# Block products of a softplus feed-forward in the second half of d_ff only, and the staging of block sums moved to other storage

## The chip, the cores and the metric

One core of a Trainium2 chip runs the whole program. The metric is the device time of one execution in microseconds; the kernel before took 651.81 us in the median of three runs (650.3 to 656.61).

## The reference, cut to what matters

The input is q, k and v of 4 batches, 8 heads, 768 positions and 64 channels, and two weight matrices, 512 x 2048 and 2048 x 512, in 64-bit floating point.

```
k_sum = k.reshape(B, H, nb, 32, D).max(axis=3)
v_sum = v.reshape(B, H, nb, 32, D).mean(axis=3)
scores = concat(masked q k^T / 8 (only |i - j| < 16), q k_sum^T / 8 + log(32))
a = softmax(scores)
x = a @ concat(v, v_sum)             # 3072 tokens x 512
h = x @ w_in                         # 512 -> 2048
out = softplus(h) @ w_out            # 2048 -> 512
```

Each row attends to its neighbours within 15 positions and to 24 block sums (maxima of keys, means of values). The result goes through a feed-forward with softplus.

## The kernel before, in words

**Tokens.** The 3072 tokens are 12 chunks of 256 (three to a batch), and two chunks make a group, so there are six groups, x = 0 to 5, of 512 tokens. Attention is done in units of one chunk and two pairs of heads, four units to a group: scores (line 643), masking and row minimum on VectorE (656), exponentials on ScalarE (664), normalizing (677 or 680), a transposition that goes by 32 x 32 squares on VectorE (710), out to DRAM (718) and back (722), and the values' product (741). The result is copied from PSUM to r (753), and r is kept in DRAM for the second pass (616). Group 0 has a path of its own, with transposition on TensorE (697) and its queries and values in the storage s0 to s3.

**Two passes over d_ff.** The 2048 hidden channels are 16 blocks f of 128. Since the weights of only half of them fit, groups 0 to 4 first run through f = 0 to 7 (first pass) and put a partial output in DRAM (1219); group 5 runs through all 16 blocks, during which the second half of the weights is loaded and converted; then groups 4, 3, 2, 1, 0 run through f = 8 to 15 (second pass), adding their partial output (1207). For the second pass the kept r is loaded again (1295).

**Precision.** Every operand is split in a high and a low part that TensorE can multiply at its full rate, and each product is three: high x high, high x low, low x high. The weights come as pairs of 32-bit words and are turned to a high and a low part by bit operations (lines 934 to 977), eight steps to a tile, partly in temporaries.

**Hidden products, two ways.** Plain (`hidden`, 1051): per block f, 4 parts of 128 input channels x 3 terms = 12 matmuls of 512 columns (1060). As blocks (`hidden_pair`, 1077): two f blocks and the two chunks make a 2 x 2 matrix of 2 x 2 blocks, multiplied with seven products in place of eight. Each product is 2 x 3 = 6 matmuls of 256 columns (1100), 42 for a pair of f against 24 of 512 columns. For that, sums of weight blocks are made once per pair of f (`sums_of_weights`, 983: lines 1000, 1008 to 1011, 1024, 1031; four sums, then high and low part, storage s0 to s3), seven operands are made for each group (`prepare`, 848: four differences, 811 and 812, and seven splits, 796 and 803), and the products are combined by a copy p (1119 or 1120) and seven additions or subtractions on VectorE (1110). A pair holds both PSUM banks of the ring "ph" until its softplus has read them; a plain hidden product takes one of these two banks, and so does the values' product of an attention unit (735).

`WHOLE = 2` says from which group on the first pass works as blocks: groups 0 and 1 are plain (`prepare_whole`, 815: high and low part of r, 827 and 834), groups 2 to 5 and the whole second pass are as blocks. This makes 16 plain blocks f and 40 pairs.

After either, softplus is taken twice by ScalarE from PSUM (1162 rounded to the high part gh, 1166 exact), VectorE makes the low part gl (1170), and 12 matmuls of 512 columns per f add to the output (1177).

**Storage.** Tiles are taken from rings by tag. The ring "t" has two buffers and holds, in the order of use, key and value rows for block sums (`Sums.declare`, 369: kf and st, four loads of 384 KB each per batch), temporaries of the weights, temporaries of the weights' sums, and outputs on their way out. s0 to s3 hold group 0's queries and values, then some temporaries of weights and one tile of group 1, then the weights' block sums.

**Order.** Every piece of work is a task with a number, given in the order in which the program adds tasks. `SEQUENCE` (147) lists these numbers in the order in which they are issued; a letter picks another engine for a task. Each engine and the DMA queue of SyncE works its tasks strictly in that order, and a task waits for its operands and for its storage.

Of the kernel before, what the change touches and what calls it, by code (L numbers as in the profile page):

```python
# [147 lines left out]
162 163a 0 1 3 4 5 6 7 8 64 153 154a 2 313 43 155 156 164 165 157 51 68 9 10 11 12 13 14 15 16 17 18 19 158a 20 21 22  # L148
23 24 45 44 46 53 47 152 25 167 55 166 69 49 26 159 27 28 29 30 160 31 171 32 33 34 168 57 35 161a 169 36 37 52 38 72
59 73 39 40 54 48 180 86 87 61 170a 56 58 100 74 104 75 50 172 76 88 189 60 77 173 41 79 78 70 181 89 315 314 66 174  # L150
65 182 62 80 90b 63 175 71 67 101 321 312 176 316 183 198 199 106 185 105 184 108 109 103 107 42 177 110 122 190 194
123 191 111 112a 192 102 124 193 81 91 93 324 92 186 187a 94 343 82 95 136 325 178 84 125 179 85 83 96 345 98 99 195
97 196a 113 326 126 140a 146a 200a 204 188 327 197 201 202 203 205 115 342 208 114 116 117 344 137 328b 127 346 372
374 351a 129 329 138 118 128 354 119 130 317 355 236 213 120 131 132 320 322 134 133 121 330 135 390 375 209a 246 373
210 211 389 356 357 376 247 255 393 248 212 217 331 391 249 143a 392 250 256 251 332 377 257 218 252 206 214 262 147a
318 319 207 215a 358b 398 333 263 237 401 258 359 259 264 265 402 334 253 266 323 219a 254 378 227 382 238a 260 220
221 403 139 222 360 261 239 335 420 419 269 270 240 216a 241 336 267 268 421 347 352 242 348 404 149 228a 276 271 379a
232 384 272 422 383a 229 380 405b 349 274 277 230 338 350 231 223 361 273 278 385 362 406 423 363 353 141 279 364 386
283 381 284 280 233 234 275 224 428a 235 407 431 285 340 365 533 286 534 287 394 290 225 291 532 366 537a 142 408 432
387a 409 388 411 515a 297 516a 399 243 395 298 433 226 397 410 368 400 292 396 293 369a 540 434 557 244 558 435a 281  # L160
299 300 436 282 561a 556 294 520 541 437 517a 148 412 370a 288 245 367 542 301 518a 413 417 424 289 564 427 543 429
438 425 430 440 521a 441 371a 544b 519 439 426 522 418 339a 581 589a 523a 580 582 295 296 302 583 303 304 442 545 415
584 565 416 443 341 756 445 546 446 535 447 757 760 566 567 448a 592 449 761 547 450 451 452 548 536 610 549 612 550
568 458 306a 307 611 150 144 453 309a 305 618a 613 569 459 593 538 460 310 461 308 465 539 609 466 462 524a 467 468
454 469 455 594 525 595 311 596 551 570 145 552 768 571 621 559 472 572 769 554 456 555a 526a 597 562 473 474 573 560
774 479 527a 480 574 563 553 775 475 622 476 773 598 457 481 482 463 483 575 776 486 764 777 782 585 464 588 758 623
487 624 470 591 625 488 489 586 587 599 785 590 471 765 576a 601 600 602 626 786 490 762 627 787 477 759 603 604a 802
803 493 804 606 801 500 501 763a 810 788 494 614 789a 805 766 578 579 615 767 790 607 628 495 620 502 496 617 813 629
770 619 814 616 478 630 608 484 497 631 151 503 485 414 605 815 1053 632 771 577 504 633a 640 637 635 816 643 491 641
638 642 830 644 1054 639a 492 1055 645a 791 829 831 636 646 647 337 1057 778 652 649 650 648 651 653 654 655 657 834a  # L170
772 659 784 817b 656 779 792 837 658 498 1056 661 528 818 855 660 662 444 838 663 854 859 668 499 856 783 529 669 505
670 793 507 673 1058 508 819 780 839 679 840 862 841a 509 781 997 998 842 1001 675 530 1000 843 676 506 863 674 999
682 664 510 677 864 683 511 794 680 531a 678 512a 684 795 1006 685 513a 514 665 686 688 687 1061 865 681 689 866a 693
1065 690 694 666 667 671 1009 695 867 796 797 1010 1026 1029 1027 1028 1025 672 1062 806 820 868 698 701 811 704 1011
1034 823 699a 700 702 703 822 705 709 707 807 821 812 711 710 708 1012 706 713 712 691 714 1066 1013 799a 718 719 715
808 720 809 692 696 798 824 1059 1063 1037 1014 825 832 723 726 833 725 1038 724 727 1071 729 728 1079 732 730 734
827a 828a 1074 835 844 846 735 736 733 845 836 731 847 738 737 1072 1070 739 743 740 697 716 744 745 800 1073 1015 848
869 1082 857 717 1060 1064a 858 872 721 870 871 1100 849a 1108a 861 722 741 742 1039 860 1040 826 873 1041 1042 850
851 852 853a 1103 1083 1016 1019 874 1043 876 881 884 748 878 882 883 1101 885a 879a 880a 877 886a 1017 1099 887 746
888 896 890 893 753 891 898 894 1084 897 899 750 902 889 1102 892 747 1085 900 903 751a 901 895 1086 909 1002 1111 904  # L180
910 875 1004 749 1008 911 905 1003 1018 1087 906 914 754 917 916 920 915a 918 921 1005 919 922 925 923 907 924 926
1246 755 1247 927 929 930 1007 928 931 908 934 912 935 1067 936 1020 1112 1251a 1068a 913 1021 1248 1023a 1044 1069
1030 1047 1033 939 942 940 943 1036 941 945 948 950 946 944 952 951 949 954 955 1035 1046 1032 953 1045 947 634 1031
956 959 932 960 961 933 1088 1048 1113 1075 1049a 1254 1024 1089 1270 964 967 965 1114 970 1090 1076 1092 968 966 971
1115b 752 1080 975 969 1078 973 976 974 979 977 980 937 1077 978 1274 1091 1022 938 957 1116 972 981 984 985 1081 986
1271 1117 1255 1093 1051a 1269 1050 1094a 958 1118 1052 1120 1121 1104 1119 1096 1256 1107 1277 1097 962 1257 1110
1105 963 982 1258a 1259 1278 1106 1109 1095 1122 1098a 1293 1260 1294 1296 1249 1123 1130 983 1124 1125 1295 1127 1133
1131 1128 1132 1250 1129 1134a 1126 1135a 987 1292 1261 1136 1137 1142 1145 1139 1138 1146 1279 1140 1252 1143 1147
1141 988 1301a 1148 1264 1149 991 1150 1280 989 1262 1253 1304 1151 1152 1281 990 1144 1263 1158 1153 1154 1159 1160
994 992 1265 1266 1155 995 1282 1283 1321 1323 1284 1285 1163 996 1166 993 1286 1676 1305 1169 1164a 1167 1170 1174  # L190
1172 1173 1165 1175 1324 1156 1168 1157 1306 1178 1171 1176 1177 1272 1307 1161 1179 1183 1320 1329 1308 1162 1184
1180 1185 1322 1188 1191 1275 1189 1190 1267a 1309 1192 1273 1194 1193 1195 1287 1199 1197 1200 1310 1198 1203 1268a
1201 1276 1204 1202 1196 1208 1209 1205 1181 1210 1332 1288 1297 1303 1289 1182 1311 1333 1213 1219 1214a 1216 1217
1679 1215 1334 1218 1222 1220 1224 1299 1314 1313 1335 1302 1226 1225 1223 1227 1298 1300 1677 1228 1229 1221 1336
1186 1312 1233 1234 1678a 1187 1206 1290a 1337 1230 1235 1338 1315 1316a 1207 1211 1680 1212 1231 1682 1232 1238 1325
1339 1340 1317a 1326 1681 1327 1342 1291 1318 1341 1331 1328 1330 1343 1344a 1319a 1683a 1350 1345 1236 1239 1351 1347
1348 1353 1352 1349 1354a 1355a 1346 1356 1357 1686 1362 1365 1359 1360 1243 1358 1363 1361 1820 1367 1458 1369 1476
1366 1240 1684 1368 1370 1371 1372 1364 1378 1373 1379 1380 1237 1244a 1374 1459 1477 1383 1478 1386 1384 1385 1389
1813 1245 1481 1685a 1241 1387 1479 1460 1390 1392 1394 1388 1396 1480 1375 1376 1463 1692a 1393 1395 1398 1377 1391
1381 1695a 1482 1399 1397 1403 1494 1461 1404 1462 1400 1405 1408 1464 1483 1689 1484 1411 1410 1465 1466 1551a 1409a  # L200
1412 1495a 1414 1382 1417 1816 1552a 1499 1467 1415 1413 1242 1419 1472 1468a 1496 1485 1418 1421 1401 1420 1422 1402
1416 1423 1406 1428 1497 1407 1553 1424 1498 1469 1429 1554 1425 1430 1433 1490 1513 1555 1503 1470 1504 1514a 1436
1435 1434 1439 1500 1501 1471 1502a 1486a 1518 1515 1516 1442 1437 1505a 1440 1444 1438 1441 1445 1443 1426 1487 1446
1532 1448 1517 1810 1427 1449 1506 1519 1447 1431 1450 1453 1454 1455 1568 1571 1556a 1520 1569 1570 1507 1574 1572
# [40 lines left out]
def kernel(  # L245
# [33 lines left out]
    NG = 2  # L279
# [1078 lines left out]
```

## Time and profile before

| | |
|---|---|
| median of three runs | 651.81 us (650.3 to 656.61) |
| profiled execution | 652.5 us, span 650.7 us |
| mean granted TensorE clock | 0.979 |
| PE busy | 608.9 us, 94%, 4812 matmuls |
| VectorE busy | 444.8 us, 68% |
| ScalarE busy | 351.0 us, 54% |
| GpSimd busy | 199.3 us, 31% |
| DMA | 104.46 MB, mean 161 GB/s |

The span runs from the first to the last instruction. A matmul's end is modelled, so PE's busy time is more than what TensorE needs; the distance from start to start in a full stream says more. A row of a view names the line, engine, operation, the tile written and the tiles read, the count, then busy time and mean duration, and the idle time of the engine right before, with what ended it.

### The profile page before, as it was taken

What the parts mean: (1) busy time and instruction counts of PE and PEld (TensorE: products, weight loads), DVE (VectorE), ACT (ScalarE), POOL (GpSimd) and SP (SyncE); (2) the same over time, 40 slices, a digit from 0 to 9 for tenths busy, and PEclk for the clock granted to TensorE, in tenths of its full rate; (3) what the DMA queues carried; (4) which work ended last, traced back from release to release, by engine and by line L of the source; (5) the groups of instructions that cost most, each with busy time, mean ns of one, the idle gap of its engine ahead of it and who ended that gap; (6) DMA issues with size and microseconds to landing.
All of it is one profiled execution on the core that took longest, in us unless ns stands there. A gap on an engine that the chain in (4) does not pass through costs nothing.

```text
span 650.7 us, 13005 instructions
## 1 busy us (share of the span) xinstructions
PE 608.9 (94%) x4812; PEld 522.0 (80%) x4812; DVE 444.8 (68%) x1150; ACT 351.0 (54%) x852; POOL 199.3 (31%) x168
## 2 busy tenths in 40 slices
PE   8559889898999989999999999999999999999997
PEld 7357667676778778878978987889899898999895
DVE  4978799646888567686659999986655455455442
ACT  3979789694886363768525877742312313123220
POOL 5325155252741231011144474332230233401000
PEclk9979989898999989999999999999999999999999
DMA  9998997989977964686554742023102140040121
GB/s 288 265 269 245 259 236 220 266 240 259 289 246 235 231 204 129 208 252 196 165 154 138 259 156 95 1 66 130 48 17 98 65 150 14 1 130 1 53 79 64
DMA packets 88960, 104.46 MB, mean 161 GB/s; under 512 B 27488, under 2 KB 67008, under 8 KB 88128
## 3 DMA queue, kind: packets, MB, share of 16 engines
q1 hardware_dynamic: 88896, 103.62, 54.1%
q8 instruction: 38, 0.62, 0.4%
q14 instruction: 26, 0.21, 0.1%
HBM read 73.92 MB, written 27.26 MB: 156 GB/s over the span
## 4 chain that ended last, share of the span: by engine, by line
PE 60%; DMA 15%; DVE 10%; SPq 6%; ACT 4%; issue 2%; POOL 2%; DVEq 0%; POOLq 0%; ACTq 0%
PE po L1177 26%; PE hx L1100 14%; PE hy L1100 10%; PE ph L1060 3%; DMA squares<-tb 3%; DMA st<-v_hp_dram 3%; PE xo L741 2%; ACT sp L664 2%; SPq L722 2%; PE sc L643 2%; DMA v<-v_hp_dram 2%; PE warm L1251 2%; DMA raw<-w_in_dram 1%; DMA first<-v_hp_dram 1%; DMA raw<-w_out_dram 1%
## 5 line engine op out<-in xcount | busy, mean ns | idle before, releaser
L1177 PE MATMUL po<-w,gh 128*128 128x512 f32 x768 | 204.5, 394 | 1.9 <-ACT gh L1162 1.7
L1177 PEld LDWEIGHTS po<-w,gh 128*128 128x128 f32 x768 | 139.6, 188 | 31.5 <-ACT gh L1162 3.0
L1177 PE MATMUL po<-w,gl 128*128 128x512 f32 x384 | 117.1, 399 | 1.0 <-DVE gl L1170 1.0
L803 POOL TENSOR_TENSOR x<-r,x 128x512 fp32r<-128x512 f32 x35 | 48.8, 1400 | 189.6 <-DVE x L796 98.7
L1162 ACT ACTIVATE gh<-hx 128x512 fp32r<-128x512 f32 x40 | 23.9, 598 | 121.7 <-DVE hx L1110 121.6
L1177 PEld LDWEIGHTS po<-w,gl 128*128 128x128 f32 x384 | 70.4, 189 | 16.9 <-DVE gl L1170 1.8
L1100 PE MATMUL hx<-x,w 128*128 128x256 f32 x480 | 71.7, 286 | 4.2 <-ACT p L1119 3.5
L1100 PE MATMUL hx<-x,sw 128*128 128x256 f32 x480 | 71.8, 286 | 3.2 <-DVE u L1110 1.6
L1100 PEld LDWEIGHTS hx<-x,w 128*128 128x128 f32 x480 | 65.6, 190 | 10.3 <-ACT p L1119 5.0
L664 ACT ACTIVATE sp<-sp,nm 128x120 f32<-128x120 f32 x192 | 73.0, 382 | 0.2
L1100 PEld LDWEIGHTS hx<-x,sw 128*128 128x128 f32 x480 | 63.9, 191 | 5.4 <-DVE u L1110 2.5
L1100 PE MATMUL hy<-x,sw 128*128 128x256 f32 x480 | 66.5, 284 | 0.0
L963 POOL TENSOR_TENSOR t<-t,raw 128x1024 int32<-128x1024 int32 (+1 forms) x20 | 43.6, 2192 | 70.7 <-DVE t L949 31.0
L1100 PEld LDWEIGHTS hy<-x,sw 128*128 128x128 f32 x480 | 61.5, 190 | 0.6 <-DVE sw L1031 0.2
L1060 PE MATMUL ph<-xw,w 128*128 128x512 f32 x192 | 51.2, 421 | 0.0
L656 DVE CUSTOM_DVE_ANT_0 sp<-sc,added 128x120 f32<-128x120 f32 x192 | 40.8, 278 | 10.8 <-PE sc L643 9.6
L1060 PEld LDWEIGHTS ph<-xw,w 128*128 128x128 f32 x192 | 38.2, 203 | 9.7 <-DVE gl L1170 0.3
L796 ACT CAST x<-r 128x512 fp32r<-128x512 f32 x37 | 22.8, 619 | 34.2 <-PE hx L1100 11.2
L677 POOL TENSOR_TENSOR sp<-sp,ss 128x960 f32<-128x960 f32 x11 | 20.0, 1815 | 68.9 <-DVE ss L672 51.6
L1110 DVE TENSOR_TENSOR u<-hx,p 128x256 f32<-128x256 f32 x40 | 16.9, 424 | 32.7 <-ACT p L1119 27.1
L1110 DVE TENSOR_TENSOR u<-hy,u 128x256 f32<-128x256 f32 x80 | 30.9, 419 | 11.8 <-PE hy L1100 11.1
L1170 DVE TENSOR_TENSOR gl<-hy,gh 128x512 fp32r<-128x512 f32 x40 | 27.5, 688 | 13.7 <-ACT hy L1166 13.6
(108 smaller groups left out, 974.8 us busy)
## 6 DMA issues: line engine op xcount, KB each, us to landing
squares<-tb SPq DMA_DIRECT2D x20, 512.0 KB
pT<-squares SPq DMA_DIRECT2D x80, 128.0 KB
raw<-w_out_dram SPq DMA_DIRECT2D x16, 512.0 KB
kf<-kT_dram SPq DMA_DIRECT2D x16, 384.0 KB
raw<-w_in_dram SPq DMA_DIRECT2D x6, 1024.0 KB
q<-qT_dram SPq DMA_DIRECT2D x20, 256.0 KB
raw<-r SPq DMA_DIRECT2D x20, 256.0 KB
part<-ob SPq DMA_DIRECT2D x10, 512.0 KB
```

The lines of the kernel that those rows point to most:

```text
L656: nc.vector.tensor_tensor_reduce(out=sp()[:, n], in0=unit(n), in1=added()[:, kinds.index((lows[w], lows[w + 1]))], scale=-SCALE, scalar=FL ...
L664: nc.scalar.activation(sp()[:, n], sp()[:, n], AF.Exp, bias=nm()[:, n:n + 1], scale=-1.0, accum_out=ss()[:, n:n + 1],)
L677: engine.tensor_tensor(sp(), sp(), s, op=ALU.mult)
L796: copy(out=to(0), in_=a())
L803: engine.tensor_tensor(to(1), a(), to(0).bitcast(F32), op=ALU.subtract)
L963: nc.gpsimd.tensor_tensor(a, a, word(0, I32), op=ALU.add)
L1060: nc.tensor.matmul(ph(), lhsT=lhs(part, cc), rhs=xw[cc][0]()[:, xw[cc][1], a], start=cc == 0 and n == 0, stop=cc == NCC - 1 and n == 2,)
L1100: nc.tensor.matmul(to()[:, half], lhsT=lhs(wa, cc), rhs=of_x(xa)[:, cc * CH:(cc + 1) * CH], start=cc == 0 and m == 0, stop=cc == NG - 1 an ...
L1110: DVE, dve(CH), lambda: nc.vector.tensor_tensor(out(), a(), b(), op=op), reads, [write],
L1162: nc.scalar.activation(gh(), all_of(), AF.Softplus)
L1170: nc.vector.tensor_sub(out=gl(), in0=all_of(), in1=gh().bitcast(F32))
L1177: nc.tensor.matmul(po[t](), lhsT=a()[:, t * P:(t + 1) * P], rhs=w2()[:, part, i2 * DM:(i2 + 1) * DM], start=f == f0 and i == 0, stop=f == ...
```

## The change

Groups 2 to 5 do their first-pass blocks plain, and group 5 all 16 of its blocks; only the second pass of groups 4 to 0 (five groups) works as blocks. The block sums of the first half's weights are no longer made. Group 5 isn't copied to r: its high and low parts are taken from PSUM, as for group 0. The plain operands alternate between two sets of storage by the parity of the group. The key and value rows for the block sums move from ring "t" to s0 to s3, one buffer each, and temporaries of weights that were there move to "t" and "x0". `SEQUENCE` is replaced by a new one of 2099 tasks in place of 2348.

```diff
-    WHOLE = 2
...
-                kf = buffer([P, S], F32, "kf", "t", T_BUFS, dynamic=True)
-                st = buffer([P, n_t, P], F32, "st", "t", T_BUFS, dynamic=True)
+                kf = buffer([P, S], F32, "kf", tag=f"s{i % 2}", pool=wts, bufs=1)
+                st = buffer([P, n_t, P], F32, "st", tag=f"s{2 + i % 2}", pool=wts, bufs=1)
...
-        if x not in x_bufs and not x:
+        if x not in x_bufs and not x % 2:
             x_bufs[x] = [(buffer([P, 1, 2, CT], F32R, "xw", tag=f"x{3 + cc}", bufs=1), 0) for cc in range(NCC)]
         elif x not in x_bufs:
-            x_bufs[x] = [(buffer([P, 1, 2, CT], F32R, "xw", tag=f"x{1 + cc}", bufs=2), 0) for cc in range(NG)]
-            both = buffer([P, NG, 2, CT], F32R, "xw", tag="s3", pool=wts, bufs=1)
-            x_bufs[x] += [(both, g) for g in range(NG)]
+            x_bufs[x] = [(buffer([P, 1, 2, CT], F32R, "xw", tag=f"x{1 + cc % 2}", bufs=2), 0) for cc in range(NCC)]
...
-        if x:
+        if x and x < NX - 1:
             r = block(2 * i + hp // NG)
...
-            (1, 0): ("tb", work, 1), (1, 1): ("x0", work, 2), (2, 0): ("x0", work, 2),
-            (2, 1): ("s0", wts, 1), (3, 0): ("s1", wts, 1), (3, 1): ("s2", wts, 1),
+            (1, 0): ("x0", work, 2), (2, 0): ("x0", work, 2), (3, 0): ("x0", work, 2),
...
-        pairs = x >= WHOLE or f0 > 0
+        pairs = f0 > 0
...
                 if x < NX - 1:
                     keep(x, n, r[n])
-                if x < WHOLE:
                     prepare_whole(x, n, r)
-                else:
-                    prepare(x, n, r)
...
-        if x == WHOLE and not f0:
-            for f in range(0, HALF, 2):
-                sums_of_weights(f)
-        if x == NX - 1:
-            sums = attend(x, sums)
-        elif x and not f0:
+        if x and not f0:
             sums = attend(x, sums)
```

More of the change, by code (lines that the diff above doesn't have):

```diff
@@ L153 @@
[L153 to L162, printed above, removed]
@@ L233 @@
[L233 to L234 removed]
[6 rows of a table removed]
+0 3 4 162 43 1 5 6 51 7 44 8 9 10 11 12 13 14 15 16 17 18 19 20 21 22 23 24 25 26 27 28 29 30 31 32 33 153 45 47 68
+154a 158a 34 155 163a 64 46 52 156 53 55 164 2 157 165 167a 72 54 35 57 189 69 36 159 59 160a 161 49 73 48 37 86 313
+61 166 56 74 171 87 190 38 39 168 75 58 40 191 88 41 60 104 62 100 76a 172a 50 152 321a 180 192 176a 77 79 66 316 65
@@ new lines @@
+173 174 63 67 169 42 78 108 71 175 80 170 70 177 314 315 185 194 101 109 89 312 193 110 122 123 81 324 208 198 181a
+103 90b 124 107 105 343 111 82 195 84 344 182 209a 91 102 136 106 196a 112a 346 183 199 184 92 93 94 95 325 83 213
+178a 197 85 342 113 125 326 372 345 96 186 210 211 114 179 351 212 138 115 116 98 117 99 97 376 126b 127 317 118 120
+327 214 200a 129 128 215a 130 354 137 217 131 373 246 218 380 328 329 134 330 140 132 121 141 355 133 320 119 135 201
+247 319 356 248 390 255 249 392 393 331 223a 357 187 389 334 332 318 374 322 333 391 202 204 250 256 257 188 262 203
@@ new lines @@
+412 437 524 541 546a 424 370 543 426 300 244a 438 288 341a 525 245 147a 440 289 301 429 427 441 295 339 413 439 549
+430 296 425 526 567 417 369 527 303 568 569 305 570 528 550 304 529 442 697 518 415 522 309 443 416a 302 447a 371a
+418a 571 445a 448 446 576a 519 551 521 530 142 533 552 306a 449 450 532 553 451 458 531 459 452 453 554 579 597 598
+600 307 599 460 601 454 699 455 555 456 695 461 580 606a 465 466 581 694 467 462 534 609 711 698 714 556 310a 457 535a
+558 713 544 582 144 696 468 719a 710 583a 584 463 610 559 469 611 537 612 464 705 470 548 700 557 712 547 613a 545 414
@@ new lines @@
+986 873 976 1120 1117 874 1115 1100 1013 869 692 870 875 988 876 765 1014 1000 1003 913 1123 946a 989a 1101 993 1140
+1016 945 851 1015 857 915a 1427 917a 1428 1561 877 1562 858 864 865 871 872 994 1102 991a 878 1017 1002 1103a 1005
+1143 1001 992 947a 1104 1124 1006 881 1018 1148a 880 879 1563 1019a 990 1142 1105 1021a 1022a 1125 882a 1023a 1433
+1139 1024 1141 1025 1026 1094 1027 1028 1151 1034 1029 1035 1095 1030 1041 1567 1042 883 1167 1036 1106 1107 1037 1043
+1109 1038 1168 1020 1108 1048 1170 1097 1126 1127a 1044 1049 1098 1050 1051 885 1045 1110 1128 1031 1113 1111 1171
@@ new lines @@
+1169 886a 1118 1129 1052 1130 1152 1153 1112 1114 1131 1032 1122 1033 1055 1154 1056 1062 1057 943 1133 1119 1155 1058
+1063 1039 1132 1040 1429a 1046 1176 1179 1156 887 1121 1064 1437 1059 1134 1047 1065 1157 1066 1180 1135 1181 1182
+1183a 884 1137 1144 1150 1158 1160 1136 1146 1145 1149 1053 1069 1161 1159 1147 1070 1054 1060 1071 1072 1434 1138
+1162 1184 1163 1073 1061 1185 1076 1165 1571 1077 1078 1166 1440 1441a 1067 1068 1079 1080 1172 1173 1186 1568a 1074
+1075 1081 1085a 1187 1164 1174 1084 1083 1177 1188 1178 1175 1438 1088 1439a 1442 1189 1190 1193 1191 1194 1082 1192
@@ new lines @@
+1086a 1087 1195 1196 1197 1198 1204 1205 1206 1089 1199 1207 1253 1254 1208 1574 1211 1200 1212 1271 1272 1218 1219
+1276 1201 1213 1273 1214 1289 1220 1221 1274 1255 1202 1215 1225 1203 1275 1277 1278 1226 1256 1257 1258 1222 1232
+1262 1290 1227 1233 1291 1279a 1209 1228 1210 1259 1216 1260 1261 1308 1263a 1292 1264 1267 1346 1294 1234 1235 1229
+1293 1347a 1295 1296a 1217 1265 1309a 1266 1223 1310 1280 1268 1224 1298 1299 1313 1239 1236 1430 1300a 1281 1240 1230
+1241 1282 1701 1311 1242 1285 1231 1312 1283 1269 1246 1348a 1243 1284 1247 1237 1248 1238 1249 1314 1090 1327 1250
@@ new lines @@
+1541 1539 1540 1542 1534 1499 1696 1546 1500 1572a 1576 1519 1543 1547 1520 1548 1579a 1581 1582 1573 1697a 1583 1589
+1585 1584a 1586 1592 1524 1587 1588 1593 1594 1590 1596 1595 1591 1597 1598 1605 1705 1525 1544 1545 1549 1702 1703a
+1599 1600 1606 1607 1704 1610 1611 1616 1613 1550 1612 1614 1615 1617 1618 1619 1552 1620 1554 1551 1558 1623 1555
+1621 1622 1601 1624 1625 1559 1626 1630 1602 1603 1835 1829 1627 1631 1699 1604 1632 1608 1635 1708a 1711a 1638 1636a
+1639 1641 1637 1646 1640 1642 1839 1556 1644 1647 1645 1648 1650 1649 1643 1609 1651 1655 1656 1652 1657 1700 1628
@@ new lines @@
+1872 1893 1892 1894 1895 1898 1899 1900 1903 1906 1904a 1905 1909 1907 1908 1912 1910 1914 1913 1915 1918 1916 1919
+1876 1877 1911 1917 1920 1923 1924 1925 1976a 1896 1968 1928 1931 1929 1934 1930 1932 1939 1828 1980a 1933 1941 1937
+1982a 1897 1974a 1935 1940 1901 1977 1938 1978 1943 1936 1955 1902 1921 1983 1975a 1944 1942 1984a 1948 1981a 1945
+1949 1950 1985 1988 1987 1986a 1824 1989 1991 1996 1922 1990 1998 1959 1994 1992 1999 1995 1997 1993 2000 2001 1926
+1927 2002 2007 2008 2009 1946 2012 2013 1947 1952 1957 2018 2015 2014 1951 2016 2019 2023 2021 1953 2017 1956 2020
@@ L241 @@
+2022 2025 1954 2003 2024 1960 2004 2026 1961 2027 2028 2032 2033 2029 2005 2006 2034 2037 2040 2039 2038 2041 2043
+2046 2048 2042 2044 2047 2050 1958 1962 2045 2049 2010 2011 2051 2052 2053 2054 2057 2030 2058 2059 2062 2065 2063a
+2068 2064 2066 2067 2031 2073 2071 2069 2075 2074 2072 2077 2078 2076 2079 2035 2036 2070 2082 2089 2083 2084 2094
+2055 2056 2060 2061 2080 2081 2088 2087 2085 2086 2096 2098 2095 2091 2097 2090 2093 2092
 """
```

117 lines of the change are left out of this document (40 added, 77 removed), and 6 rows, old and new, of the table SEQUENCE.

## The prediction

> **What bounds the kernel now.** I read the granted clock and the busy time by stretches first, cut at the places where the kind of work changes: start and first attention (to 53 us), the feed-forward of token groups 0 and 1 (to 172), groups 2 to 4 (to 340), the first half of group 5 (to 430), the dense part (to 632), the tail. The columns are the stretch, its length, PE, PEld, DVE, ACT and POOL busy with their instruction counts, the granted clock, the DMA engines' busy share and GB/s.
>
> ```profile
> core 0: us, PE busy (x) PEld busy (x) DVE busy (x) ACT busy (x) POOL busy (x), PEclk, DMA share, GB/s
> 0.00:53.00 53.00, 38.06 (x573) 30.53 (x574) 36.96 (x142) 36.94 (x126) 21.78 (x37) 0.87 0.98 264
> 53.00:172.00 119.00, 108.41 (x868) 84.40 (x869) 88.42 (x260) 92.64 (x252) 48.73 (x39) 0.96 0.92 253
> 172.00:340.00 168.00, 160.00 (x1487) 137.85 (x1487) 119.45 (x366) 101.44 (x281) 43.63 (x33) 0.99 0.70 206
> 340.00:430.00 90.00, 86.21 (x548) 74.86 (x549) 82.85 (x144) 64.88 (x90) 42.38 (x28) 1.00 0.36 123
> 430.00:632.00 202.00, 202.00 (x1282) 183.03 (x1282) 111.74 (x234) 52.91 (x101) 42.82 (x33) 1.00 0.20 67
> 632.00:650.70 18.70, 14.23 (x64) 11.36 (x62) 5.34 (x9) 2.18 (x4) 0.00 (x0) 1.00 0.15 57
> ```
>
> From 430 to 632 us TensorE never stops, at full clock: there only the amount of matmul work counts. Before 53 us the DMA engines are full (0.98). Between, TensorE has some idle time everywhere, while VectorE reaches 82.85 of 90 us in the fourth stretch. So a change of matmul work is paid in full at the end, and can be paid out of idle time between 53 and 430 us.
>
> How much time is there to be had? Busy time of PE has modelled ends, so I count matmuls and multiply by their spacing in full streams, read from the chain of waits in order of time (start us, length us, what, how many) and, for the scores, from the timeline:
>
> ```profile
> 118.38 5.93 PE ph L1060 x18
> 125.01 4.13 PE ph L1060 x18
> 256.07 1.11 PE xo L741 x32
> 471.35 1.43 PE hx L1100 x12
> 472.78 1.43 PE hy L1100 x12
> ```
>
> ```profile
> 223.87 1.05 PE L643 MATMUL sc<-k,q 64*64 64x120 f32 x32
> ```
>
> A 512-column product takes 4.13 / 18 = 0.229 us, a 256-column block product 1.43 / 12 = 0.119 us, a unit of 32 value products 1.11, a unit of 32 score products 1.05. The first row is the same work just after a wait: 1.8 us more, so a gap of TensorE costs more than its own length. The counts of two stretches, PE alone (count, busy and mean ns, idle before and its releasers):
>
> ```profile
> L1060 PE MATMUL ph<-xw,w 128*128 128x512 f32 x192 | 51.2, 421 | 0.0
> L1177 PE MATMUL po<-w,gh 128*128 128x512 f32 x112 | 30.2, 399 | 1.7 <-ACT gh L1162 1.7
> L1177 PE MATMUL po<-w,gl 128*128 128x512 f32 x52 | 16.0, 402 | 0.5 <-DVE gl L1170 0.5
> L741 PE MATMUL xo<-pT,v 120*64 120x64 f32 x256 | 10.1, 237 | 5.8 <-DMA pT<-squares 2.1 <-DMA st<-v_hp_dram 1.4 <-DMA raw<-r 1.2
> L643 PE MATMUL sc<-k,q 64*64 64x120 f32 x256 | 9.5, 271 | 2.6 <-DMA k<-kT_dram 1.9 <-DMA q<-qT_dram 0.6
> ```
>
> 53 to 172 us: (192 + 112 + 52) x 0.229 = 81.5, 8 units of values 8.9, 8 of scores 8.4: 98.8 of 119 us. Lost: 20.2 us, and the waits named are the attention's (DMA), not the feed-forward's.
>
> ```profile
> L1177 PE MATMUL po<-w,gh 128*128 128x512 f32 x321 | 85.4, 395 | 0.1
> L1177 PE MATMUL po<-w,gl 128*128 128x512 f32 x164 | 49.6, 401 | 0.5 <-DVE gl L1170 0.5
> L1100 PE MATMUL hx<-x,w 128*128 128x256 f32 x243 | 37.0, 288 | 4.2 <-ACT p L1119 3.5 <-DVE u L1110 0.5
> L1100 PE MATMUL hx<-x,sw 128*128 128x256 f32 x240 | 36.8, 289 | 3.2 <-DVE u L1110 1.6 <-DVE hx L1110 1.4 <-DVE x L803 0.2
> L1100 PE MATMUL hy<-x,sw 128*128 128x256 f32 x240 | 34.2, 286 | 0.0
> L1100 PE MATMUL hy<-x,w 128*128 128x256 f32 x120 | 18.0, 286 | 0.8 <-DVE u L1110 0.4 <-DVE hy L1110 0.3
> L741 PE MATMUL xo<-pT,v 120*64 120x64 f32 x384 | 14.3, 225 | 2.4 <-DMA pT<-squares 1.5 <-DMA v<-vs 0.7
> L643 PE MATMUL sc<-k,q 64*64 64x120 f32 x320 | 10.5, 269 | 0.6 <-DMA q<-qT_dram 0.6
> ```
>
> 172 to 430 us: 485 x 0.229 = 111.1, 843 x 0.119 = 100.3, 12 units of values 13.3, 10 of scores 10.5: 235.2 of 258 us. Lost: 22.8 us. Of this, 4.2 + 3.2 + 0.8 = 8.2 us are idle times directly before a block product, nearly all waiting for the copies and sums that block products need (p, u, hx, hy); the attention's waits are only 3.0.
>
> **The change, part by part.** *More matmul work.* 20 of 40 pairs of f blocks (groups 2, 3, 4 with four each, group 5 with eight) become plain. A pair as blocks is 7 products of 6 matmuls, 42 x 0.119 = 5.0 us; plain it is 2 x 12 of 512 columns, 24 x 0.229 = 5.5 us. 20 x 0.5 = **+10.0 us**, on the engine that sets the end. The Trainium skill, "TensorE: Matmul & The Clock Gate", section "Back-to-back issue gap", gives N / 2.4 + 2.5 ns for a matmul in a warm stream: by that, as an estimate, a pair is 42 x 109 = 4.6 against 24 x 216 = 5.2 us, the 20 pairs cost +12, and the time would come out 2 us above my forecast. The same section gives 131 ns per matmul at N = 512 within a real kernel, by which a plain pair would be the cheaper one (24 x 131 = 3.1 us); the 229 ns above contradict it, and I give it no chance.
>
> *Waits that go.* The same 20 pairs lose their combining: seven VectorE operations a pair at line 1110 and one copy of p. All of them lie before 430 us (columns: stretch, length, DVE busy, clock, DMA share, GB/s):
>
> ```profile
> 172.00:340.00 168.00, 34.10 (x84) 0.99 0.70 206
> 340.00:430.00 90.00, 22.52 (x56) 1.00 0.36 123
> ```
>
> 140 operations, 56.6 us of VectorE, and the 8.2 us of waiting for them go with certainty, as no plain product reads p, u, hx or hy. What is late next is the softplus (line 1162) ahead of the output products; in the plain stretch above it cost 1.7 + 0.5 us over 16 blocks.
>
> *Elementwise work that changes.* Groups 2 to 5 are no longer prepared as seven operands with four differences, but as four whole tiles. What is added, 24 halves from r and 8 straight from PSUM (high, low):
>
> ```profile
> L827 ACT CAST xw<-r 128x256 fp32r<-128x256 f32 x7 | 2.7, 403 | 0.1
> L834 DVE TENSOR_TENSOR xw<-r,xw 128x256 fp32r<-128x256 f32 x4 | 1.6, 421 | 0.1
> L771 ACT CAST xw<-xo 128x256 fp32r<-128x256 f32 x8 | 2.8, 376 | 1.7 <-PE xo L741 1.5
> L775 DVE TENSOR_TENSOR xw<-xo,xw 128x256 fp32r<-128x256 f32 x8 | 2.9, 413 | 0.0
> L803 DVE TENSOR_TENSOR x<-r,x 128x512 fp32r<-128x512 f32 x28 | 23.1, 833 | 3.1 <-ACT x L796 3.0
> L811 DVE TENSOR_TENSOR r<-r 128x512 f32<-128x512 f32 x20 | 13.4, 693 | 3.2 <-ACT r L753 2.5 <-POOL x L803 0.4
> L1031 DVE TENSOR_TENSOR sw<-ws,sw 128x1024 fp32r<-128x1024 f32 x5 | 7.1, 1429 | 0.0
> ```
>
> 32 x 0.82 = 26 us are added. Removed are 28 lows at 0.83 or more, 28 highs and 16 differences at 0.69: over 45 us. Four of the eight sets of weight sums (before group 2) go too, each about 1.4 for its low half and more for sums and high half. The chain from the last attention unit of a group to the first hidden product becomes copy, high, low: about 0.6 + 0.4 + 0.4 us, where a block group runs through splits and differences at 0.7 to 0.8 each. And in the fourth stretch the sums of the second half's weights are no longer due within group 5, but one group later, under the dense part.
>
> *The staging.* k and v rows for the sums of batches 1 to 3 leave the ring "t" (two buffers, shared with weight temporaries and stores) for s0 to s3. DMA counts and bytes don't change, nor does what SP issues, only when buffers come free. Now this row stands in the chain of waits:
>
> ```profile
> 45.80 6.98 DMA st<-v_hp_dram
> ...
> 67.72 11.23 DMA st<-v_hp_dram
> ...
> 93.45 0.35 ACT k L525
> ```
>
> The second load was issued only at 67.7, when the ring and SP's order let it. With the DMA engines at 0.92 a load freed earlier pushes another back, so I bound the gain of this and of the missing weight sums in the second stretch between 0 and 8 us and take **-3**. In the other direction, s0 to s3 hold the first group's queries and values until about 53 us, so the first load can come up to 53 - 45.8 = 7 us later than now; its sums are first copied at 93.45, some 40 us on, which hides that as long as the four rounds of loads don't each slip.
>
> *The sum for 172 to 430 us.* Lost there: 22.8. From below 8.2 come back (the waits named); from above 22.8 less the attention's 3.0 and about 2 for the softplus, 18. I take **-15**, nearer to the upper end, because the remaining 14.6 are mostly short slips before products whose operands the saturated VectorE delivers late, and VectorE loses 56.6 us of work in these 258. The start, dense part and tail stay: 0. The written order is a new one throughout; I put nothing on that beyond these bounds.
>
> Sum: +10.0 - 3 - 15 = -8.0 us. The profiled execution took 652.5 us (span 650.7, and 1.8 around it); 652.5 - 8.0 = **644.5 us**. The three runs have a median of 651.81, 0.7 below the profiled one; within that I make no difference. Against the median it is -1.1%; a measurement of this kernel tells about 1% from no change, and that is the bound of my three chances (645.3 and 658.3 us).
>
> **The rivals.** (1) *Only the named waits go* (8.2), nothing comes back from 53 to 172: +10.0 - 8.2 = +1.8, 654.3 us. For it: DMA at 0.92 and 0.70 feeds the attention, whose chain alone could set the pace of groups 2 to 4. Against: TensorE, not DMA, is at 160 of 168 there. Chance 0.25.
>
> (2) *Plain groups run like the plain stretch* (slower). The only plain stretch now gets 98.8 us of products into 119, a share of 0.83. If groups 2 to 4 go at that share, their 168 us, with about 153 of products now (counted as above) and 6 more after, take 159 / 0.83 = 192: +24; with +4 and -6 for group 5, +22, 674 us. The mechanism is attention units on TensorE's queue, whose late pT blocks the hidden products queued behind them. It decides once the DMA share in that stretch nears 0.9; half way it makes 663 us. Against: bytes are the same and the share is 0.70. Chance 0.15.
>
> (3) *All that can come back does*: +10.0 - 8 - 18 = -16, 636.5 us. For it: the relief of VectorE is larger than all of TensorE's loss. Against: loads wait for loads in the second stretch. Chance 0.15.
>
> That the change doesn't do what it says I rule out: `pairs = f0 > 0` is false for all of group 5 too.
>
> **How the numbers follow.** My forecast has 0.45, its own range 640 to 649. It lies on the bound of 1%, about two thirds of it below 645.3. Faster: 0.30 + 0.15 = 0.45; same: 0.15 + 0.22 = 0.37; slower: 0.15 and 0.03 of rival 1 = 0.18. The range reaches from below rival 3 to near the half way case of rival 2: 634 to 661.
>
> **What would show it.** In the changed profile: ph x672 and block products x840 in all; 24 hidden matmuls of a plain pair in about 5.5 us; line 1110 x140 in place of 280; no idle before a hidden product on ACT p or DVE u before the second pass; group 5's stretch without gaps; lost time between first hidden product and dense part down from 43 to about 25 us. It is wrong if that loss stays above 35 us (then the attention set it), or if a plain pair takes other than 5.5 us in a full stream, or if the waits named before output products (line 1177) grow by several us.

## The result, and the profile after

The changed kernel took 629.92 us (median of four runs, 628.99 to 630.68), the kernel before in the same runs 653.95 us: a ratio of 0.9636, 95% interval 0.9577 to 0.9694. The profiled execution took 630.05 us with a span of 628.3 us. The prediction had 644.5 us and a range of 634 to 661: the direction was right, the time lies 4 us below the range, and the gain is nearly three times the one forecast (22.4 us of span in place of 8.0).

The line of busy times on the changed kernel's page, and the busy time by stretches, cut at the same events as before: the first hidden product of the feed-forward, the first of group 2, the first of group 5, the begin of the second pass, the end of the dense part. The columns are those of the prediction.

```profile
PE 609.2 (97%) x4452; PEld 508.9 (81%) x4452; DVE 388.0 (62%) x998; ACT 328.0 (52%) x809; POOL 162.0 (26%) x145
```

```profile
0.00:52.00 52.00, 41.16 (x573) 32.92 (x573) 37.87 (x139) 35.67 (x123) 20.35 (x36) 0.80 1.00 285
52.00:164.00 112.00, 109.30 (x927) 86.04 (x926) 83.18 (x256) 87.01 (x238) 36.79 (x30) 1.00 0.88 252
164.00:324.00 160.00, 158.98 (x1254) 127.65 (x1253) 79.60 (x275) 96.82 (x273) 31.74 (x33) 1.00 0.77 228
324.00:406.00 82.00, 82.00 (x357) 66.66 (x356) 66.50 (x87) 52.36 (x71) 30.57 (x17) 1.00 0.37 127
406.00:610.00 204.00, 204.00 (x1291) 184.77 (x1290) 116.01 (x238) 53.97 (x102) 42.53 (x32) 1.00 0.19 66
610.00:628.30 18.30, 13.75 (x60) 10.91 (x58) 4.87 (x9) 2.18 (x4) 0.00 (x0) 0.99 0.16 57
```

Read against the lines of before: in groups 0 and 1 TensorE is now at 109.30 of 112 us (108.41 of 119), in groups 2 to 4 at 158.98 of 160, in group 5 at 82.00 of 82. Group 5 is without a gap and VectorE has 66.50 of 82 us there, where it had 82.85 of 90.

What TensorE lost is counted as in the prediction, from PE alone in the two stretches, groups 0 and 1 first, then groups 2 to 5 (count | busy and mean ns | idle before and its releasers):

```profile
L1045 PE MATMUL ph<-xw,w 128*128 128x512 f32 x192 | 47.2, 396 | 2.1 <-DVE gl L1155 2.0
L1162 PE MATMUL po<-w,gh 128*128 128x512 f32 x126 | 34.4, 400 | 0.0
L1162 PE MATMUL po<-w,gl 128*128 128x512 f32 x63 | 19.3, 399 | 0.0
L629 PE MATMUL sc<-k,q 64*64 64x120 f32 x288 | 9.7, 270 | 0.5 <-DMA k<-kT_dram 0.5
L727 PE MATMUL xo<-pT,v 120*64 120x64 f32 x256 | 9.4, 225 | 0.1
```

(192 + 126 + 63) x 0.229 = 87.2, 8 units of values 8.9, 9 of scores 9.5: 105.6 of 112 us. Lost: 6.4 us, before 20.2.

```profile
L1045 PE MATMUL ph<-xw,w 128*128 128x512 f32 x480 | 116.7, 394 | 0.0
L1162 PE MATMUL po<-w,gh 128*128 128x512 f32 x306 | 80.5, 394 | 0.0
L1162 PE MATMUL po<-w,gl 128*128 128x512 f32 x150 | 45.2, 399 | 0.0
L727 PE MATMUL xo<-pT,v 120*64 120x64 f32 x384 | 13.8, 225 | 0.1
L629 PE MATMUL sc<-k,q 64*64 64x120 f32 x288 | 9.5, 269 | 1.0 <-ACT gh L1147 1.0
```

936 x 0.229 = 214.3, 12 units of values 13.3, 9 of scores 9.5: 237.1 of 242 us. Lost: 4.9 us, before 22.8.

So the span's -22.4 us is made up of +10.0 for matmuls, -13.8 of lost time in groups 0 and 1, -17.9 in groups 2 to 5, and -1.0 in the start (first hidden product at 51.9 us in place of 52.9); 0.3 is the error of this count.

### The profile page after: what moved, and what is told of

Same layout as the page of the kernel before. It is cut to its first block, busy times and chain, and to the rows that moved or that the text cites. A ratio compares the mean times of both kernels' runs of the same rounds, so it can differ in the third digit from the quotient of the medians.

```text
span 628.3 us, 12022 instructions
## 1 busy us (share of the span) xinstructions
PE 609.2 (97%) x4452; PEld 508.9 (81%) x4452; DVE 388.0 (62%) x998; ACT 328.0 (52%) x809; POOL 162.0 (26%) x145
## 4 chain that ended last, share of the span: by engine, by line
PE 85%; DMA 8%; SPq 3%; ACT 1%; DVE 1%; issue 1%; DVEq 0%; POOL 0%; POOLq 0%; ACTq 0%
PE po L1162 40%; PE ph L1045 21%; PE hx L1085 9%; PE hy L1085 7%; PE xo L727 3%; PE sc L629 3%; DMA raw<-w_in_dram 2%; DMA k<-kT_dram 2%; DMA squares<-tb 2%; PE warm L1236 2%; DMA kf<-kT_dram 1%; DMA q<-qT_dram 1%; DMA v<-v_hp_dram 1%; SPq L708 1%; SPq L523 1%
## 5 line engine op out<-in xcount | busy, mean ns | idle before, releaser
L1045 PE MATMUL ph<-xw,w 128*128 128x512 f32 x672 | 163.9, 395 | 2.1 <-DVE gl L1155 2.0
L1045 PEld LDWEIGHTS ph<-xw,w 128*128 128x128 f32 x672 | 125.6, 188 | 32.5 <-DVE gl L1155 2.8
L1147 ACT ACTIVATE gh<-hx 128x512 fp32r<-128x512 f32 x20 | 12.0, 599 | 114.9 <-DVE hx L1095 114.9
L1155 DVE TENSOR_TENSOR gl<-ph,gh 128x512 fp32r<-128x512 f32 x56 | 38.0, 684 | 40.8 <-ACT ph L1151 39.3
L1147 ACT ACTIVATE gh<-ph 128x512 fp32r<-128x512 f32 x56 | 33.5, 598 | 53.4 <-PE ph L1045 48.5
L650 ACT ACTIVATION_READ_ACCUMULATOR sp<-sp,nm 128x1 f32 x192 | 36.0, 187 | 0.0
L1085 PE MATMUL hx<-x,sw 128*128 128x256 f32 x240 | 35.4, 283 | 0.0
L1085 PE MATMUL hx<-x,w 128*128 128x256 f32 x240 | 35.1, 282 | 0.0
L1085 PEld LDWEIGHTS hx<-x,w 128*128 128x128 f32 x240 | 32.8, 189 | 1.9
L1085 PE MATMUL hy<-x,sw 128*128 128x256 f32 x240 | 33.2, 282 | 0.0
L1151 ACT ACTIVATE ph<-ph 128x512 f32<-128x512 f32 x56 | 32.8, 591 | 0.0
```

Of the source, the lines that this page charges most:

```text
L650: nc.scalar.activation(sp()[:, n], sp()[:, n], AF.Exp, bias=nm()[:, n:n + 1], scale=-1.0, accum_out=ss()[:, n:n + 1],)
L1045: nc.tensor.matmul(ph(), lhsT=lhs(part, cc), rhs=xw[cc][0]()[:, xw[cc][1], a], start=cc == 0 and n == 0, stop=cc == NCC - 1 and n == 2,)
L1085: nc.tensor.matmul(to()[:, half], lhsT=lhs(wa, cc), rhs=of_x(xa)[:, cc * CH:(cc + 1) * CH], start=cc == 0 and m == 0, stop=cc == NG - 1 an ...
L1147: nc.scalar.activation(gh(), all_of(), AF.Softplus)
L1151: nc.scalar.activation(all_of(), all_of(), AF.Softplus)
L1155: nc.vector.tensor_sub(out=gl(), in0=all_of(), in1=gh().bitcast(F32))
```

## The experiments

**The price of a plain pair.** The changed kernel with its second pass plain as well, so that 20 more pairs give up their block products.

```diff
-        pairs = f0 > 0
+        pairs = False
```

The preparation and the weight sums of the second pass go with them.

> The changed kernel with the second pass plain too, so 20 more pairs are plain; no block sums of weights at all. The second pass is a full stream of TensorE, so this measures the price of a plain pair by itself. My prediction's step (0.5 us a pair from the spacing): 640 us, +10. By the formula N / 2.4 + 2.5 ns: 642 us. If a plain pair costs TensorE nothing more: 630 us or less.

642.8 us, 12.9 over the changed kernel; the spans are 641.4 and 628.3 us. 2.1 of these 13.1 us lie ahead of the second pass, which begins at 408.1 us in place of 406.0. From there to the end it takes 233.3 in place of 222.3 us: 11.0 us for 20 pairs, 0.55 each, or a little less, as by the spacing of the products under 1 us of it is lost time. The prediction's 0.5 from the spacing of the products is confirmed to within a tenth. In the dense part nothing hides it. The Trainium skill's formula in "TensorE: Matmul & The Clock Gate", section "Back-to-back issue gap", gave 12 for the same 20 pairs, as an estimate; that section gives it for an isolated matmul with a warm clock, not for a stream. The measurement lies between the two.

**Order alone, or work alone.** Each kernel with the other one's written order, carried over task by task; a task that only one of them has was put beside its neighbour.

> The changed kernel with the written order of before carried over task by task (a plain hidden product stands where the block products of its pair stood). If less elementwise work is what brought TensorE's lost time down (theory 1), the time stays at 630 to 637 us and the loss between the first hidden product and the dense part at 10 to 17 us. If the new written order did it (theory 2), the time is 645 to 655 us and the loss from 53 to 172 us stays near 20 us. If the staging did it (theory 3), 630 to 637 us too.

> The kernel before with the written order of the changed one carried over (block products and their combining stand where the plain hidden products stand, preparation right behind its operands). Theory 2 (order): the loss from 53 to 172 us falls from 20 to below 10 us and the time to 640 us or less, as nothing is plain that wasn't. Theory 1 (less work): 650 to 665 us, since the work is all there and the order is not made for it.

The new work in the old order took 987.33 us (ratio 1.5156, 1.5096 to 1.5217), the old work in the new order 907.79 us (1.393, 1.3878 to 1.3983). The waits of PE in the first of them (us in total, times, longest):

```profile
PE ph L1045 <- DVE gl L1155: 85.6, 9, 19.7
PE sc L629 <- DVE nm L642: 32.0, 5, 10.9
PE ph L1045 <- ACT r L739: 30.6, 3, 15.7
```

A hidden product waits up to 19.7 us for a gl that comes late. Every time expected of these two kernels was missed by more than 240 us. Neither order was good for the work that it wasn't written for; so these two runs can't say what either half of the change is worth.

**One planner for both works.** Hence each work got an order written anew by one and the same planner, with the same effort. First with a planner that took VectorE's and GpSimd's durations as independent of each other, then with one that let them hold each other up. "Stage" is the changed kernel with k and v rows staged in ring "t" again.

> The changed kernel with a written order of my own (a list planner of engine and DMA times with a random search over priorities, started from its own order). It is the yardstick for the two runs beside it. All theories: 626 to 638 us.

> The kernel before with an order from the same planner and the same search time, started from its own order; the work is unchanged. Theory 1 (the work itself): the waits for p, u, hx and hy and the loaded VectorE stay, 645 to 655 us. Theory 2 (its written order was the poorer one): 630 to 641 us, and the loss from 53 to 172 us drops from 20 to under 10 us.

> The changed kernel with the staging undone (key and value rows again in the ring t, the weights' temporaries where they were before), with an order from the same planner and search time. Theory 3 (staging): 6 to 12 us above the yardstick, in the first 172 us. Otherwise within 3 us of it.

> The changed kernel in an order from a better planner (it now also counts that VectorE and GpSimd hold each other up). Yardstick for the two beside it: 620 to 645 us.

> The kernel before in an order from the same planner, same search time. If the work itself makes the difference: 10 us or more above the yardstick. If only the written order did: within 4 us of the yardstick.

> The changed kernel with the staging undone, in an order from the same planner, same search time. If the staging matters: 6 to 12 us above the yardstick. If not: within 4 us.

Both planners fell short of what was expected of the changed kernel (626 to 638 us, then 620 to 645). The first planner's orders, each searched from the kernel's own order, took 699.67 us (changed), 721.79 (before) and 693.12 (stage): poor orders, and staging in the ring even the best of them, so they decide little. The second planner's took 664.61 us (ratio 1.0194, 1.0149 to 1.0239), 703.76 (1.0796, 1.0744 to 1.0848) and 671.94 (1.0318, 1.0271 to 1.0365). With equal effort for the order, the work of before is 39 us worse, although it has 10 us less of matmuls. That speaks for the work as what carries the gain, and against a lucky order; but none of these orders comes near the one of the change, and a planner's miss of a few us in one of them isn't to be told from the work. The stretch of groups 0 and 1, from the first hidden product to the first of group 2, is 121.8 us long for the changed work (52.3 to 174.1) and 134.3 for that of before (48.6 to 182.9); with the first planner's orders it is 124.8 (62.7 to 187.5) and 135.8 (51.2 to 187.0).

**Staging.** The changed kernel's own order, with only what had to be moved for staging in ring "t":

```diff
-                kf = buffer([P, S], F32, "kf", tag=f"s{i % 2}", pool=wts, bufs=1)
-                st = buffer([P, n_t, P], F32, "st", tag=f"s{2 + i % 2}", pool=wts, bufs=1)
+                kf = buffer([P, S], F32, "kf", "t", T_BUFS, dynamic=True)
+                st = buffer([P, n_t, P], F32, "st", "t", T_BUFS, dynamic=True)
```

> The changed kernel with only the staging undone: key and value rows for the block sums again in the ring t, the temporaries of the weights again where they were before, the order otherwise that of the changed kernel. Theory 3 (staging): 640 to 650 us, lost mostly from 53 to 172 us. Theories 1 and 2: 629 to 633 us.

692.79 us (1.0634, 1.0591 to 1.0677). That is an upper bound at most: temporaries of weights moved as well, and the order didn't fit any longer. The loss was expected mostly in groups 0 and 1 and isn't there: the first hidden product begins 7.7 us later (59.6), that stretch is 2.8 us longer (114.9), and groups 2 to 4 take 49 us more (209.0). In the second planner's pair staging is worth 7.3 us, but most of it lies in the start, ahead of every feed-forward (the first hidden product comes at 60.9 in place of 52.3 us). The waits of PE in that kernel:

```profile
PE xo L727 <- DMA first<-v: 8.8, 1, 8.8
PE ph L1046 <- DVE gl L1156: 7.7, 2, 6.5
PE vt L428 <- DMA vn<-v_hp_dram: 6.8, 1, 6.8
```

Two of the three are loads of the first batch's values, which lie outside the ring; there the order of the loads decides. From the other side, the kernel before was given a third buffer in the ring (and three in place of four for gl, to make room):

```diff
-    T_BUFS = 2
+    T_BUFS = 3
```

> The kernel before with three buffers in ring t in place of two (paid for by three in place of four of gl), in its own written order, in which only a few tasks had to move. If the ring t held up the loads and, through SyncE's strict order, the attention (theory 3): 640 to 647 us. If the written order already fits two buffers, as loads are listed where the ring is free: 649 to 654 us.

> The same with three buffers in ring t and three of gl, in the order of the run with three such buffers. That run began group 2 at 168.5 us in place of 173.0 and group 5 at 338.8 in place of 342.5, and ended where before ended. If it gave the gain back to a VectorE that was full from 340 to 430 us, the gain shows here: 3 to 5 us below the run without the third buffer. If the ring t does nothing: the same time within 2 us.

654.79 us in ten runs (1.0034, 0.9999 to 1.0069): no gain. Nor did the third buffer help once combining was out (next): 646.44 against 643.85 us. Some 2 us of this is the price of the missing gl: from the first product of the second pass to the end both kernels with three gl take 223 us (222.9 and 223.0), both with four 221.0. Even so, the order of before gains nothing from more room in the ring that these runs could tell. What the staging itself is worth in the order of the change stays open: with the ring, group 2 begins 10.5 us later in the kernel above (174.5 in place of 164.0) and 10.3 later in the second planner's pair (184.4, 174.1), but only 1.9 in the first's (189.4, 187.5). In the first two of these most of it is lost ahead of the first hidden product, which in the kernel before, with the ring too, came at 52.9.

**Combining and weight sums taken out of before.** The order kept exactly; the copy p and the seven VectorE operations of the 20 first-pass pairs left out (line 1110), and in a second kernel the first half's weight sums as well.

```diff
+        combined = f >= HALF and x < NX - 1
...
-        combine(u2, half(z, 1), p1, ALU.add, [(z, 1), p1], u2)
+        if combined:
+            combine(u2, half(z, 1), p1, ALU.add, [(z, 1), p1], u2)
```

> The kernel before, its written order kept task for task, but in the 20 pairs of the first pass and of group 5 the copy p and the seven combining operations are left out (softplus reads the products as they are, so part of the computation is missing). 160 tasks less, matmuls unchanged. Theory 1 (the combining cost it): most of the 22.8 us lost from 172 to 430 us come back, 630 to 638 us. Only the 8.2 us of waits that the prediction names: 643 us. Theory 2 (the written order): 645 to 651 us.

> The kernel before in its own written order, without the combining of the 20 pairs (as in the run without combining) and without the block sums of the first half's weights (those block products read the weights themselves, so part of the computation is missing). 177 tasks less, matmuls unchanged. If the weight sums are what loses time from 53 to 172 us (theory 1 for that stretch): group 2 begins by 166 us and the time is 632 to 638 us. If that loss belongs to the written order: group 2 begins at 170 to 174 us as in the other runs in this order, and the time is 641 to 646 us.

643.85 us (0.9883, 0.9826 to 0.994), and without weight sums 643.71 (0.9885, 0.9829 to 0.994). Group 5, cut at the same events: the kernel before, then the one without combining:

```profile
342.50:430.00 87.50, 83.71 (x511) 72.69 (x510) 81.56 (x143) 64.25 (x89) 42.38 (x28) 1.00 0.37 124
```

```profile
336.10:419.50 83.40, 80.91 (x509) 71.91 (x508) 68.40 (x86) 61.94 (x82) 44.30 (x28) 1.00 0.37 130
```

VectorE's share falls from 0.93 to 0.82, as low as in the changed kernel (66.50 of 82 us, 0.81), but the stretch is only 4 us shorter and TensorE still has gaps in it, where the changed kernel has none. The gain of 7.7 us is about the 8.2 of waits named in the prediction, and no more; leaving out the weight sums gives nothing beyond the noise of some 4 us. With the order of before, the relief of VectorE is not passed on; as I read it, each engine still comes to its next task in the old sequence, whose pace other waits set. From here to the changed kernel it is 643.71 - 629.92 = 13.8 us, and 10 to 11 more that the plain pairs cost: some 24 us of lost time that neither combining nor weight sums explain by themselves. Which of the rest brings them (preparation as whole tiles, other storage, staging, the order) was not separated.

**VectorE's load put into the changed kernel.** The order kept, and additions of 128 x 256 that read scratch and that nobody waits for, behind the hidden products of the 20 plain pairs:

```diff
+                if x >= 2 and f % 2:
+                    load_vector(x, f)
...
+        for _ in range(7):
+            order.add(DVE, dve(CH), lambda: nc.vector.tensor_tensor(to(), a(), b(), op=ALU.add), [a, b], [to])
```

Besides the kernel with seven for each pair, one has them further back in VectorE's list (behind the pair's last gl), one has three for each pair, and one has seven in group 5 alone.

> The changed kernel with its order kept and seven VectorE additions of 128x256 (SBUF to SBUF, on scratch, no one waits for them) added behind each of the 20 pairs that became plain: the combining's load without its dependences. If load on VectorE delays everything else on it: 640 to 655 us. If it was the dependences (TensorE waiting for p and u) and not the load: 630 to 633 us.

> The changed kernel with its order kept, and the same 140 VectorE additions of 128 x 256 that nobody waits for as in the run before (7 for each of the 20 plain pairs of groups 2 to 5, some 59 us of VectorE), now placed in VectorE's list behind the low part gl of the pair's second block in place of right behind its hidden products. Nothing of the computation changes. Theory 'load' (VectorE's amount of work sets the pace of the first pass, wherever it stands): as in the run before, 652 to 662 us. Theory 'place' (the additions cost only where gl stands behind them in the queue): 630 to 642 us, and no wait of output products for gl longer than 3 us.

> The changed kernel with its order kept, and 3 in place of 7 such additions behind the hidden products of each of the 20 plain pairs, 60 in all, some 25 us of VectorE. Nothing of the computation changes. Theory 'proportional' (every microsecond of VectorE costs half a microsecond, as in the run with 140): +12 us, 640 to 644 us. Theory 'slack' (the order holds a reserve, which 25 us don't use up): 630 to 635 us. Theory 'place' says the same as slack: 3 additions hold gl back by 1.3 us.

> The changed kernel with its order kept, and 7 such additions behind the hidden products of each of the 8 pairs of group 5 alone, 56 in all, some 24 us of VectorE; groups 2 to 4 have none. Nothing of the computation changes. In the run with 140, the stretch from group 5's first hidden product to the second pass grew from 82.3 to 99.1 us, and the groups before it from 108.7 to 118 us. Theory 'group 5 is the tight place': +15 to +18 us, 645 to 648 us. Theory 'even': +8 to +12 us, 638 to 642 us. Theory 'slack': below +5 us.

| kernel | time, us | groups 2 to 4, us (added VectorE busy) | group 5, us (added VectorE busy) | VectorE's share in group 5 |
|---|---|---|---|---|
| changed | 629.92 | 160.0 (0) | 82.0 (0) | 0.81 |
| three a pair | 636.90 | 161.9 (20.8) | 86.8 (18.1) | 0.92 |
| seven, group 5 | 648.38 | 158.6 (0) | 99.4 (31.8) | 0.93 |
| seven a pair | 658.04 | 170.7 (42.2) | 99.1 (32.7) | 0.94 |
| seven, further back | 665.59 | 170.4 (38.4) | 98.5 (29.6) | 0.91 |

The shares come from the rows of that stretch; of the changed kernel it stands above, and of the other four in the table's order:

```profile
326.00:412.80 86.80, 84.39 (x358) 67.73 (x357) 79.45 (x110) 51.21 (x71) 28.49 (x17) 0.98 0.34 118
```

```profile
326.50:425.90 99.40, 87.97 (x358) 69.38 (x356) 92.06 (x142) 51.09 (x69) 28.35 (x17) 0.95 0.29 103
```

```profile
335.20:434.30 99.10, 86.82 (x357) 68.43 (x355) 92.82 (x142) 51.07 (x69) 28.25 (x17) 0.97 0.29 104
```

```profile
334.00:432.50 98.50, 87.14 (x357) 68.51 (x355) 90.09 (x135) 51.07 (x69) 28.66 (x17) 0.97 0.30 104
```

In group 5 VectorE's load costs little up to about nine tenths; from there on it sets the length of the stretch, at 0.91 to 0.94 busy, and TensorE's clock falls below 1.00 with the gaps (0.95 over 99.4 us is 5 us of clock by itself). The kernel before stood at 81.56 of 87.5 = 0.93 there: at that bound. One difference stays: these additions read SBUF alone and take longer beside GpSimd (last section), which the combining, reading PSUM, doesn't do; what part of the price that is wasn't separated. The wait behind it, PE's in the kernel with seven in group 5 (first row), beside that of the changed kernel (second fence):

```profile
PE ph L1048 <- DVE gl L1171: 10.7, 6, 4.3
```

```profile
PE ph L1045 <- DVE gl L1155: 2.0, 2, 1.2
```

gl reads the PSUM bank that the hidden product after next needs; a late gl holds up the bank, and TensorE's queue behind it. "Place" is refuted: the additions cost as much in both stretches behind gl as ahead of it (170.4 and 98.5 against 170.7 and 99.1 us), and the kernel with them further back loses another 9 us at the begin of the second pass (49.4 in place of 40.4 us for its first group), where its last additions run into the first combining. "Load" is right in kind, though its 652 to 662 us was too low for this kernel, and the 640 to 655 us for the kernel with seven a pair were too low as well. Three a pair cost 7.0 us, between "proportional" (12) and "slack" (up to 5). Group 5 is the tight place: 18.5 us for its eight pairs, 17.4 of them within the stretch, where the 12 pairs of groups 2 to 4 cost 170.7 - 160.0 = 10.7.

## Why the prediction was wrong in size, point by point

- *+10 for 20 plain pairs*: right, some 11 measured. A plain pair's 24 hidden matmuls stand in the chain of the changed kernel (start us, length us) as the prediction's last part asked:

```profile
110.29 5.58 PE ph L1045 x24
...
129.42 5.55 PE ph L1045 x24
```

- *The waits for p, u, hx, hy go* (8.2): right. No combining is left ahead of the second pass (VectorE at line 1095, the columns of the stretches with DVE alone), and taking it out of before gave 7.7 us:

```profile
52.00:406.00 354.00, 0.00 (x0) 1.00 0.71 212
406.00:628.30 222.30, 56.52 (x140) 1.00 0.19 65
```

- *-15 for groups 2 to 5, of which the softplus keeps some 2*: right in kind and 2.9 too small; 17.9 came back, the upper bound of 18 nearly in full. The reason given, short slips behind a saturated VectorE, is half shown for group 5: in the new order 31.8 us put back on VectorE make the stretch 17.4 us longer, but in the old order taking the combining off shortened it by 4 us only. For groups 2 to 4 it is shown that VectorE's load costs time (10.7 us for 42.2), though VectorE is busy for only half of that stretch. Some 2 us of the 17.9 are the clock, 0.99 from 172 to 340 us before (1.7 us) and 1.00 after.
- *-3 for groups 0 and 1, "between 0 and 8 us"*: this is the step that failed; 13.8 us came back. It was bounded with "the DMA engines at 0.92, a load freed earlier pushes another back". Two things were left out of it. The first is the clock. The 20.2 us were counted against products at full clock, but the granted clock of that stretch was 0.96, and 0.04 x 119 = 4.8 us; in the changed kernel it was 1.00. In the kernel before it fell to 0.50 three times for 3.4 us (from 91.4, 118.7 and 156.3 us). The second time came right behind a wait for k, which landed at 117.9 us. These rows are the two runs of 18 hidden matmuls in the prediction's chain; the clock stands third from the end:

```profile
118.38:124.31 5.93, 5.93 (x20) 4.71 (x20) 3.02 (x6) 3.43 (x9) 3.17 (x3) 0.71 0.88 247
125.01:129.14 4.13, 4.13 (x19) 3.38 (x19) 3.98 (x20) 1.56 (x3) 0.00 (x0) 1.00 0.92 256
```

  The prediction saw these 1.8 us more and didn't put their like into the term. Five kernels go by the order of before: the two whose clock was 1.00 from 53 to 172 us began group 2 at 168.5 and 170.4 us, the three with 0.96 or 0.97 at 173.0 to 175.4.

  The second is that a load pushed back can leave the stretch. DMA moves at the same rate in both kernels (253 GB/s, share 0.92, then 252 and 0.88), and so the shorter stretch holds less: 119 x 253 = 30.1 MB before, 112 x 252 = 28.2 MB now. The rest went ahead of it (53 x 264 = 14.0, now 52 x 285 = 14.8 MB) and behind it (168 x 206 = 34.6, now 160 x 228 = 36.5 MB). The 1.9 MB are 7.5 us at that rate, nearly as much as the stretch got shorter. So the changed kernel doesn't refute that the queue was near its limit before; it refutes that the loads stay in the stretch. How near the limit was isn't shown: the kernel before with a third buffer moved 263 GB/s there. SyncE's queue changed too; its waits of before from 53 to 172 us, then of the changed kernel from 52 to 164:

```profile
SPq L378 <- DMA part<-ob: 4.2, 1, 4.2
SPq L722 <- DMA squares<-tb: 4.1, 2, 3.2
SPq L535 <- DMA raw<-w_in_dram: 3.3, 1, 3.3
SPq L518 <- DMA st<-v_hp_dram: 3.1, 3, 1.7
SPq L518 <- PE xo L741: 2.6, 2, 1.8
SPq L386 <- POOL vs L395: 2.0, 1, 2.0
```

```profile
SPq L497 <- PE sc L629: 7.2, 3, 2.7
SPq L708 <- DMA squares<-tb: 6.7, 5, 3.0
SPq L506 <- PE xo L727: 5.0, 4, 3.2
```

  Before, the queue stood still for a store of outputs, for weights and for block sums as well as for attention, with attention's loads behind; now what it waits for most is attention's own progress. What of the change brought this about is not settled. Not the weight sums alone (without them the kernel before reached group 2 at 175.4 us, in place of 173.0), not a third buffer (168.5, and 173.9 with combining out), and not the new order without the new work (907.79 us). Under the two planners the stretch is 11.0 and 12.5 us shorter with the new work. I take from this that the seven operands of group 2 and what was free to be reordered with them made room; that is argued, not shown, and the staging could have had a part in it.
- *Elementwise work*: 26 us added against over 45 removed is borne out in sum, but not on VectorE: its busy time fell by 444.8 - 388.0 = 56.8 us, no more than the combining. Other elementwise work moved to it in the new order; the relief shows on ScalarE (351.0 to 328.0) and GpSimd (199.3 to 162.0), where weight sums and copies p went too.
- *The staging at no cost, as s0 to s3 come free late*: no cost is to be seen, group 2 begins at 164.0 us in place of 173.0. Whether it brought a gain stays open, as above.
- *The written order, "nothing beyond these bounds"*: too little. With the order of before kept, leaving out the combining gave 8 us, less than the 10 to 11 that the plain pairs cost. Some 24 us of lost time went only with the new work and an order written for it, in one.
- *Rivals*: "only the named waits go" is about what happened where the order was kept; "plain groups at the plain stretch's share of 0.83" fell with that share itself, now 105.6 / 112 = 0.94 by the count of products; "all that can come back does" (636.5) was the nearest, and its 8 for groups 0 and 1 was still too small.

## What to carry to other kernels

Price the matmuls by their spacing and pay them in full, but bound what an idle engine can get back by its whole lost time, its clock included, not by the waits that a profile names: here those were what went with the order kept. In group 5 here, VectorE near 0.9 busy meant that the stretch had its length from it, wherever in its list the work stood. A share of 0.92 on the DMA engines was no bound on its stretch, since 1.9 MB could leave it: ask which loads and stores must move there. And when a change takes work away, write the order anew before judging it.

## What the runs showed of the hardware

The same 128 x 256 addition on VectorE takes very different times when both operands are in SBUF. Two groups of one shape in the kernel with seven additions a pair, the added ones and the combining, which reads PSUM (duration in ns: min/median/max):

```profile
L1137 DVE TENSOR_TENSOR u<-p,u x140: 373/425/2565, 168.6 to 426.5; 128x256 f32<-128x256 f32 x140
L1101 DVE TENSOR_TENSOR u<-hy,u x40: 411/424/425, 437.7 to 635.7; 128x256 f32<-128x256 f32 x40
```

119 of the 140 ran with no GpSimd operation beside them and took 424 ns in the mean, none more than 429; the other 21 had one beside them for a part or all of their time and took 1162. So the 140 cost 74.9 us of VectorE and not 140 x 0.425 = 59.5. The Trainium skill, "SBUF — State Buffer", section "SBUF: two separate sides", has the rule: a VectorE operation with two SBUF inputs and a GpSimd operation that reads SBUF lock each other out for a whole instruction. The trace agrees: the 40 additions from PSUM never exceed 425 ns, though 7 of them had a GpSimd operation beside them. The first planner ignored this; in its order of the changed kernel VectorE is busy for 448.9 us and GpSimd for 191.6, in the order of the change for 388.0 and 162.0. Part of the difference is another division of tasks between the engines, which was not separated.
